# Scores with 64-row contraction: a second transpose and quadrant-to-quadrant copies by DMA, in an attention and feed-forward kernel

## The chip, the cores and the metric

The kernel runs on one core of one Trainium2 chip. The metric is the time of one execution on the device in microseconds (us). The other engines named here are VectorE (DVE), ScalarE (ACT), GpSimd (POOL) and SyncE (SP), which issues most of the DMAs; TensorE is PE, and its weight loads are PEld.

Ratios are the mean time of one kernel's fast runs over the mean of the other's fast runs of the same rounds, so they are not quite the ratio of the medians quoted beside them. A bracket after a ratio is its 95% interval.

## The reference

```python
# q, k, v: [8 batches, 8 heads, 576, 64]; w_in [512, 2048], w_out [2048, 512]
q_d, k_d, v_d = (mean over 4 neighbouring positions of q, k, v)      # 144 positions
out_down  = softmax(q_d @ k_d.T / 8) @ v_d, each row repeated 4 times
out_local = softmax(q @ k.T / 8 where |i - j| < 4) @ v
x = (out_down + out_local), heads side by side                        # [4608, 512]
h = x @ w_in
return (h * sigmoid(1.702 * h)) @ w_out                               # float32
```

## The kernel before

Tokens go through the feed-forward part in nine groups of 512. A group has 64 matmuls of 128x512 on `w_in` and 64 on `w_out`. Between them, at fixed step numbers (`POS`), lies the attention of the batch that comes next, so that TensorE has dense work while the other engines prepare. "Batch 3's group" below is the group that carries the attention of batch 3; its start is the first `w_in` matmul.

A batch has two head groups of four heads. q and k of four heads lie on 128 partitions as bf16. VectorE transposes them in 32-bit units. Each unit is a pair of neighbouring bf16 values, so a head gets 32 partitions, and the pair stands in a last axis `a` of size 2. The contraction over 64 is therefore done as two accumulating matmuls over 32 rows. The downsampled q and k are pooled by GpSimd from the transposed tile.

```python
def prep_1(name, b, qd):
    store, dst = {"k": (kf, kT), "q": (qf, qT)}[name]
    tt = work.tile([128, S, 2], BF16, ...)
    t32 = tt.rearrange("p t a -> p (t a)").bitcast(FP32)
    nc.vector.transpose(out=..., in_=...)          # one of 128x576 32-bit units
    dst[b, qd] = tt

def scores(b, qd):
    for i in range(5):
        for a in range(2):
            for par in range(2):
                for r in range(4):                 # 80 matmuls of 32 rows
                    nc.tensor.matmul(sp[r // 2][...],
                        lhsT=kT[b, qd][32*r : 32*r+32, k0 : k0 + 64, a],
                        rhs=qT[b, qd][32*r : 32*r+32, q0 : q0 + 60, a],
                        start=(a == 0), stop=(a == 1), ...)
# scores_d: the same for the downsampled part, 24 matmuls of 32 rows
# ... cut ...
for g in range(n_groups):
    b = g + 1
    # ... g == 0 cut ...
    if b > 2:
        load_v4(b)                  # six DMAs on the sync queue, 192 KB each
    prep_qk(b, 0)                   # VectorE: two transposes
    pool_qk(b, 0)                   # GpSimd: k and q of head group 0
    load_qk(b + 1, ...)             # GpSimd issues four DMAs
    prep_v(b, nc.gpsimd)            # GpSimd: cast of v
    load_v(b + 1)                   # ten DMAs on the sync queue
    prep_qk(b, 1)
    pool_qk(b, 1)
    prep_v4(b, nc.gpsimd)           # GpSimd: pooling of v from v4, written to vd
    # ... mm1 and mm2 with the attention's matmuls at POS ...
```

GpSimd works through its part of one group in exactly this order. Its last result, `vd`, is read by the "AV-down" matmuls at step 42.

The softmax here doesn't subtract the row's maximum and nothing guards it: scores larger than these inputs give would overflow.

Of the kernel before, what the change touches and what calls it, by code (L numbers as in the profile page):

```python
# [8 lines left out]
FP32 = mybir.dt.float32  # L9
BF16 = mybir.dt.bfloat16  # L10
AF = mybir.ActivationFunctionType
ALU = mybir.AluOpType
# [7 lines left out]
def kernel(  # L20
# [9 lines left out]
    nc = tc.nc  # L30
    B, H, S, D = q.shape
    SD = S // 4
# [6 lines left out]
    inv_sqrt_d = 1.0 / math.sqrt(D)  # L39
    KSTART = (0, 56)  # L40
    QSTART = (0, 60)

    ctx.enter_context(
        tc.manual_schedule(engines={ET.PE, ET.Activation, ET.DVE, ET.Pool, ET.SP})
# [19 lines left out]
    eds = [persist.tile([128, 2, 464], BF16, name=f"ed{i}") for i in range(2)]  # L64
    v4 = persist.tile([128, 3, HP, 4 * D], FP32, name="v4")
    kdT = [persist.tile([128, 160, 2], BF16, name=f"kdT{i}") for i in range(NQ)]

    PA = [psum.tile([128, 2, 512], FP32, name=f"pa{i}") for i in range(3)]
    PM = [psum.tile([128, 512], FP32, name=f"pm{i}") for i in range(2)]
# [2 lines left out]
    def ps_tile(n=None):  # L72
        if n is None:
            n = turn["a"] % 3
            turn["a"] += 1
        return PA[n]
# [44 lines left out]
    def fill():  # L121
        nc.vector.memset(wz, 0.0)
        for t in kdT:
            nc.vector.memset(t[:, SD:160, :], 0.0)
        for t in vbs:
            nc.vector.memset(t[:, :, :, 64:65], 1.0)
        for t in vds:
            nc.vector.memset(t[:, :, :, 64:65], 4.0)
        for t in es:
            nc.vector.memset(t[:, :, 300:304], 1.0)  # L130
        for t in eds:
            nc.vector.memset(t[:, :, 432:464], 1.0)
# [122 lines left out]

    def prep_1(name, b, qd):
        store, dst = {"k": (kf, kT), "q": (qf, qT)}[name]
        tt = work.tile([128, S, 2], BF16, name=f"{name}T{qd}", tag=f"{name}T{qd}", bufs=1)
        t32 = tt.rearrange("p t a -> p (t a)").bitcast(FP32)
        nc.vector.transpose(  # L260
            out=t32.rearrange("p (i c) -> p c i", c=18),
            in_=store[b, qd].bitcast(FP32).rearrange("p (c d) -> p c d", c=18),
        )
        dst[b, qd] = tt

    def prep_qk(b, qd):
        prep_1("k", b, qd)
        prep_1("q", b, qd)

    def pool_qk(b, qd, names="kq"):  # L270
        for name, src in (("k", kT), ("q", qT)):
            if name not in names:
                continue
            sv = src[b, qd].rearrange("p (j f) a -> p j f a", f=4)
            t1 = work.tile([128, SD, 2, 2], FP32, name="pq", tag="pq")
            nc.gpsimd.tensor_tensor(  # L276
                out=t1, in0=sv[:, :, 0:2, :], in1=sv[:, :, 2:4, :], op=ALU.add
            )
            if name == "k":
                dst = kdT[qd][:, 0:SD, :]  # L280
            else:
                t = work.tile([128, SD, 2], BF16, name=f"qdT{qd}", tag=f"qdT{qd}", bufs=1)
                qdT[b, qd] = t
                dst = t
            nc.gpsimd.tensor_tensor(
                out=dst, in0=t1[:, :, 0, :], in1=t1[:, :, 1, :], op=ALU.add
            )

    def prep_v(b, eng, i=slice(0, 5), h=slice(0, H)):
        cp = eng.copy if eng is nc.scalar else eng.tensor_copy  # L290
        cp(out=vbs[b % 2][:, i, h, 0:D], in_=vf[b][:, i, h])  # L291
# [47 lines left out]

    def scores(b, qd, barred=False):  # L340
        sp = [ps_tile(), ps_tile()]
        if barred:
            bar_others(sp)
        for i in range(5):
            for a in range(2):
                for par in range(2):
                    for r in range(4):
                        rows = slice(32 * r, 32 * r + 32)
                        k0 = 114 * i + KSTART[par]
                        q0 = 114 * i + QSTART[par]  # L350
                        nc.tensor.matmul(  # L351
                            sp[r // 2][64 * par : 64 * par + 64, r % 2, 60 * i : 60 * i + 60],
                            lhsT=kT[b, qd][rows, k0 : k0 + 64, a],
                            rhs=qT[b, qd][rows, q0 : q0 + 60, a],
                            start=(a == 0 and not barred),
                            stop=(a == 1 or barred),
                            tile_position=(32 * r, 64 * par),
                            skip_group_check=barred,
                        )
        return sp  # L360

    def scores_d(b, qd, sd=None):
        sd = sd or ps_tile()
        bank = sd if sd is PM else [sd[:, u, :] for u in range(2)]
        for kc in range(3):
            for a in range(2):
                for r in range(4):
                    rows = slice(32 * r, 32 * r + 32)
                    j = r % 2
                    nc.tensor.matmul(  # L370
                        bank[r // 2][64 * j : 64 * j + 64, SD * kc : SD * kc + SD],
                        lhsT=kdT[qd][rows, 48 * kc : 48 * kc + 64, a],
                        rhs=qdT[b, qd][rows, :, a],
                        start=(a == 0), stop=(a == 1),
                        tile_position=(32 * r, 64 * j),
                    )
        return sd
# [428 lines left out]
    for g in range(n_groups):  # L806
        b = g + 1
        if g == 0:
            prep_qk(1, 0)
            pool_qk(1, 0)  # L810
            prep_qk(1, 1)
            load_v(1, gate=after(w_out_bf[0:1, 0, 0:1], nc.vector))
            pool_qk(1, 1)
            nc.gpsimd.tensor_copy(
                out=w_out_bf[0:1, 8, 0:1], in_=vf[1][0:1, 3, 0, 0:1]
            )
            load_w_out(2)
            load_w_out(3)
            for i in range(5):
                prep_v(1, nc.gpsimd, i=slice(i, i + 1))  # L820
            for qd in range(NQ):
                load_qk(2, qd)
            loads_2()
        elif b < B:
            if b > 2:
                load_v4(b)
            prep_qk(b, 0)
            pool_qk(b, 0)
            if b + 1 < B:
                for qd in range(NQ):  # L830
                    load_qk(b + 1, qd)
            prep_v(b, nc.gpsimd)
            if b + 1 < B:
                load_v(b + 1)
            prep_qk(b, 1)
            pool_qk(b, 1)
            prep_v4(b, nc.gpsimd)
        steps = {}
        if b < B:
            for n, f in zip(POS if g else POS_0, attention(b, None if g else (1, 2))):  # L840
                steps.setdefault(n, []).append(f)
            if g == 0:
                steps.setdefault(VDP_0, []).append(lambda: prep_vd_pe(1, PA[2]))
        gT = new_gT() if g else gT0
        mm1(g, gT, steps, 0 if g else 6)
        mm2(g, gT, {n - 16: f for n, f in steps.items() if n >= 16})
# [30 lines left out]
```

## Time and profile before

| | before |
|---|---|
| median of the runs beside the changed kernel | 332.29 us (over four runs; the first took 1751.61 us and is in this median but not in the ratio; the other three took 331.47, 331.97 and 332.61) |
| span of the profiled run | 329.5 us |
| TensorE busy | 308.0 us, 93% |
| GpSimd / VectorE busy | 138.9 us (42%) / 130.2 us (40%) |
| groups of batches 3 to 6, from start to start | 33.71, 33.53, 33.40, 34.31 us (mean 33.74) |

From the page of the kernel before come its busy times, its clock row in 40 slices (tenths of the full TensorE clock) and the shares of the chain of work that ended last.

```profile
PE 308.0 (93%) x4987; PEld 157.9 (48%) x5043; DVE 130.2 (40%) x215; ACT 184.1 (56%) x322; POOL 138.9 (42%) x168
...
PEclk9997999999999999999999999999999999999999
...
PE 87%; issue 4%; SPq 3%; ACT 2%; DVE 2%; DMA 1%; DVEq 0%; ACTq 0%
```

TensorE is the limit: it is busy nearly all the time, the clock is full except for one slice, and 87% of the chain is TensorE. The next fence is the timeline of batch 3's group, cut. Its columns are start, duration (both us), engine, line and operation, output and input; in brackets stands the idle time before it and what ended that.

```profile
102.18 11.39 PE L618 MATMUL pm<-xT,w_in_bf 128*128 128x512 bf16 x51
...
102.65 1.26 DVE L260 STREAM_TRANSPOSE kT<-kb 128x576 f32<-128x576 f32 x1
...
103.46 3.08 SPq L226 DMA_DIRECT2D v<-in_v_dram  x6
...
103.98 1.15 POOL L276 TENSOR_TENSOR pq<-kT 128x576 f32<-128x576 bf16 x1 [15.95 <-DVE kT L260]
...
107.06 0.67 POOL L285 TENSOR_TENSOR qdT<-pq 128x288 bf16<-128x288 f32 x1
...
113.50 0.84 PE L351 MATMUL pa<-qT,kT 32*64 32x60 bf16 x80
...
114.14 0.59 PE L370 MATMUL pa<-qdT,kdT 32*64 32x144 bf16 x24
...
121.22 0.84 POOL L300 TENSOR_TENSOR vd<-v 112x256 bf16<-112x256 f32 x1
...
124.61 0.32 PE L431 MATMUL pa<-vd,ed 48*64 48x65 bf16 x17
```

The matmuls that the change improves: 80 of them take 114.14 - 113.50 = 0.64 us, 8.0 ns each. GpSimd starts 1.80 us into the group, released by the first transpose, works without a gap until 122.06, and TensorE reads its last result at 124.61. The slack is 2.55 us in a group of 33.7 us.

### The profile page before, as it was taken

The page shows a single profiled execution, that of the slowest core. Times are in us where ns is not written, and L with a number is a line of the kernel's source. Part 1 is how long each engine was busy: PE and PEld are TensorE (multiplying, and loading weights), DVE is VectorE, ACT ScalarE, POOL GpSimd, SP SyncE. Part 2 cuts the span into 40 slices and gives each one's busy share as a digit, 9 for nine tenths or more (in the row PEclk, how much of TensorE's full clock was granted, in tenths as well). Part 3 has the DMA queues.
Part 4 walks back from the last instruction along what each step waited for, and adds up shares of the span by engine and source line. Part 5 has one row for each costly group of instructions (what it writes and reads, how often), then busy time and mean ns, then how long its engine had stood idle before and what let it go on. Part 6 is the DMA issues. An engine that isn't in the chain of part 4 may idle for free.

```text
span 329.5 us, 11220 instructions
## 1 busy us (share of the span) xinstructions
PE 308.0 (93%) x4987; PEld 157.9 (48%) x5043; DVE 130.2 (40%) x215; ACT 184.1 (56%) x322; POOL 138.9 (42%) x168
## 2 busy tenths in 40 slices
PE   8767999789999999999999999998999999999995
PEld 3444455445554455455544555455444544444444
DVE  4870512770468036802771277225730560000000
ACT  2552773375936683667367746674566646415611
POOL 7890844049603970298029901990098000000000
PEclk9997999999999999999999999999999999999999
DMA  7999979999814991398339922993180110011011
GB/s 126 184 188 208 171 151 183 196 210 236 191 39 132 205 207 39 116 193 171 102 100 200 200 83 86 196 195 105 40 172 2 60 41 32 2 72 56 2 62 65
DMA packets 63552, 41.36 MB, mean 126 GB/s; under 512 B 44048, under 2 KB 54416, under 8 KB 63504
## 3 DMA queue, kind: packets, MB, share of 16 engines
q1 hardware_dynamic: 55056, 26.95, 35.8%
q0 software_dynamic: 8304, 13.63, 23.9%
q8 instruction: 39, 0.64, 0.9%
q14 instruction: 9, 0.07, 0.1%
q10 hardware_dynamic: 144, 0.07, 0.1%
HBM read 44.83 MB, written 9.44 MB: 165 GB/s over the span
## 4 chain that ended last, share of the span: by engine, by line
PE 87%; issue 4%; SPq 3%; ACT 2%; DVE 2%; DMA 1%; DVEq 0%; ACTq 0%
PE pm L618 35%; PE pm L674 33%; PE pa L351 3%; SPq L214 3%; PE pa L618 2%; PE pa L431 2%; PE pa L409 2%; PE pa L370 2%; PE pa L458 2%; PE pa L674 2%; DMA vf<-in_v_dram 1%; PE pm L689 1%; PE pa L484 1%; ACT vd L321 0%; PE pa L312 0%
## 5 line engine op out<-in xcount | busy, mean ns | idle before, releaser
L618 PE MATMUL pm<-xT,w_in_bf 128*128 128x512 bf16 x528 | 120.3, 380 | 1.4 <-DVE xT L561 0.7
L674 PE MATMUL pm<-w_out_bf,gT 128*128 128x512 bf16 x493 | 114.1, 379 | 5.4 <-issue 5.2
L629 ACT ACTIVATE gT<-pm 128x512 bf16<-128x512 f32 x136 | 81.0, 598 | 45.2 <-PE pm L618 45.2
L618 PEld LDWEIGHTS <-w_in_bf 128*128 128x128 bf16 x576 | 55.8, 98 | 68.4 <-issue 2.5
L674 PEld LDWEIGHTS <-gT 128*128 128x128 bf16 x560 | 51.7, 98 | 59.5 <-issue 0.2
L276 POOL TENSOR_TENSOR pq<-kT 128x576 f32<-128x576 bf16 x16 | 18.5, 1157 | 105.0 <-DVE kT L260 96.1
L395 DVE TENSOR_TENSOR es<-es,mask 128x600 bf16<-128x600 bf16 x28 | 20.6, 749 | 92.0 <-ACT es L381 91.2
L659 ACT ACTIVATE osb<-pm 128x512 f32<-128x512 f32 (+2 forms) x35 | 20.7, 592 | 40.2 <-PE pm L674 36.1
L534 ACT COPY od<-pa 128x384 f32<-128x384 f32 (+1 forms) x56 | 18.4, 412 | 32.4 <-DVE y L444 18.7
L444 DVE TENSOR_TENSOR y<-pa,rc 128x896 bf16<-128x896 f32 x32 | 34.9, 1092 | 1.1
L555 DVE TENSOR_TENSOR xT<-pa,od 128x570 bf16<-128x570 f32 x28 | 21.1, 753 | 12.0 <-ACT od L534 11.9
L381 ACT ACTIVATE es<-pa 128x600 bf16<-128x600 f32 x32 | 19.8, 668 | 7.0 <-PE pa L351 6.8
L297 POOL TENSOR_TENSOR v<-v 112x512 f32<-112x512 f32 x18 | 22.8, 1265 | 0.0
L661 DVE TENSOR_SCALAR osb<-pm 128x128 f32<-128x128 f32 x1 | 0.3, 292 | 55.3 <-ACT osb L659 55.3
L260 DVE STREAM_TRANSPOSE kT<-kb 128x576 f32<-128x576 f32 x16 | 20.0, 1249 | 2.0 <-DMA kb<-in_k_dram 2.0
L260 DVE STREAM_TRANSPOSE qT<-qb 128x576 f32<-128x576 f32 x16 | 19.8, 1239 | 0.9 <-DMA qb<-in_q_dram 0.7
L276 POOL TENSOR_TENSOR pq<-qT 128x576 f32<-128x576 bf16 x16 | 18.4, 1148 | 0.0
L291 POOL CAST vb<-vf 128x2560 bf16<-128x2560 f32 (+1 forms) x11 | 17.6, 1618 | 0.0
L442 DVE RECIPROCAL rc<-pa 128x14 f32<-128x14 f32 x32 | 7.7, 240 | 21.7 <-PE pa L431 21.7
L351 PE MATMUL pa<-qT,kT 32*64 32x60 bf16 x1280 | 14.0, 203 | 1.5 <-issue 1.5
L351 PEld LDWEIGHTS <-kT 32*64 32x64 bf16 x1280 | 11.8, 104 | 6.7 <-issue 5.5
L300 POOL TENSOR_TENSOR vd<-v 112x256 bf16<-112x256 f32 x18 | 13.7, 759 | 1.4
(90 smaller groups left out, 247.0 us busy)
## 6 DMA issues: line engine op xcount, KB each, us to landing
vf<-in_v_dram SPq DMA_DIRECT2D x80, 128.0 KB, 4.7
out_dram<-osb SPq DMA_DIRECT2D x35, 256.0 KB, 2.1
v<-in_v_dram SPq DMA_DIRECT2D x36, 192.0 KB, 6.1
kb<-in_k_dram POOLq DMA_DIRECT2D x16, 288.0 KB, 6.8
qb<-in_q_dram POOLq DMA_DIRECT2D x16, 288.0 KB, 7.1
w_out_bf<-in_moe_w_out_dram POOLq DMA_DIRECT2D x4, 512.0 KB, 12.1
w_in_bf<-in_moe_w_in_dram POOLq DMA_DIRECT2D x2, 512.0 KB, 5.7
w_in_bf<-in_moe_w_in_dram POOLq DMA_DIRECT2D x1, 1024.0 KB, 10.7
```

The costliest lines, as they stand in the source:

```text
L260: nc.vector.transpose(out=t32.rearrange("p (i c) -> p c i", c=18), in_=store[b, qd].bitcast(FP32).rearrange("p (c d) -> p c d", c=18),)
L276: nc.gpsimd.tensor_tensor(out=t1, in0=sv[:, :, 0:2, :], in1=sv[:, :, 2:4, :], op=ALU.add)
L297: eng.tensor_tensor(out=t1[0:112], in0=x[:, :, 0:2, :], in1=x[:, :, 2:4, :], op=ALU.add)
L351: nc.tensor.matmul(sp[r // 2][64 * par : 64 * par + 64, r % 2, 60 * i : 60 * i + 60], lhsT=kT[b, qd][rows, k0 : k0 + 64, a], rhs=qT[b, qd] ...
L381: nc.scalar.activation(out=es[2 * qd + u][:, :, 0:300], in_=sp[u][:, :, 0:300], func=AF.Exp, scale=inv_sqrt_d,)
L395: nc.vector.tensor_tensor(out=ev, in0=ev, in1=mask, op=ALU.mult)
L444: nc.vector.tensor_tensor(out=y, in0=ov[:, :, :, 0:D], in1=rc.to_broadcast([128, 2, 7, D]), op=ALU.mult,)
L555: eng.tensor_tensor(out=sub(xT[hp], t0 + 3, (57, 2), (114, 5), (1, 57)), in0=sub(x, 3, (509, 2), (57, 5), (1, 57)), in1=sub(od, 3, (57, 2) ...
L618: nc.tensor.matmul(acc, lhsT=w_in_bf[:, dmc, ffc * 128 : (ffc + 1) * 128], rhs=xT[dmc][:, g * TG : g * TG + TG], start=(dmc == 0), stop=(d ...
L629: nc.scalar.activation(out=gT[:, ffc, :], in_=acc, func=AF.Silu, scale=GELU_SCALE)
L659: eng.activation(out=osb, in_=ap, func=AF.Copy, scale=1.0 / GELU_SCALE)
L674: nc.tensor.matmul(ops[t], lhsT=gT[:, ffc, t * 128 : (t + 1) * 128], rhs=w_out_bf[:, ffc, :], start=(ffc == 0), stop=(ffc == n_ffc - 1),)
```

## The change

The intent is to contract over 64 rows at once, with half as many score matmuls. From batch 2 on each q/k tile is transposed twice into two planes. In plane 0 the odd elements of heads on even quadrants, and in plane 1 the others, are brought into the neighbouring quadrant of 32 partitions by small DMAs that write one bf16 element off, so that position `a = 0` holds even elements in one quadrant and odd elements in the next: 64 rows for one head.

```diff
+    ROWS64 = 2
     def prep_1(name, b, qd):
-        tt = work.tile([128, S, 2], BF16, ...)
-        nc.vector.transpose(...)
-        dst[b, qd] = tt
+        n = 2 if b >= ROWS64 else 1
+        tt = work.tile([128, 2, S, 2], BF16, ...)
+        for x in range(n):
+            nc.vector.transpose(...)               # the same, into tt[:, x]
+        if n == 2:
+            for x in range(2):
+                f = tt[:, x].rearrange("p t a -> p (t a)")
+                for r in range(2):
+                    src = 64 * r + 32 * x
+                    to = 64 * r + 32 * (1 - x)
+                    nc.sync.dma_start(
+                        out=f[to : to + 32, 0 : 2 * S - 1], in_=f[src : src + 32, 1 : 2 * S]
+                    )
+        dst[b, qd] = tt if n == 2 else tt[:, 0]
     # pool_qk: same sizes, reads a = 0 of both planes (so it waits for the copies); pq has 1 buffer, not 2
     # scores:   40 matmuls of 64 rows in place of 80 of 32
     # scores_d: 12 matmuls of 64 rows in place of 24 of 32
     # ... cut ...
             prep_v(b, nc.gpsimd)
+            prep_qk(b, 1)
             if b + 1 < B:
                 load_v(b + 1)
-            prep_qk(b, 1)
             pool_qk(b, 1)
```

Per batch this adds four transposes and 16 copies of 71.9 KB, 96 copies in all, on the sync queue.

More of the change, by code (lines that the diff above doesn't have):

```diff
@@ L66 @@
     kdT = [persist.tile([128, 160, 2], BF16, name=f"kdT{i}") for i in range(NQ)]
+    kdP = [persist.tile([128, 2, 160], BF16, name=f"kdP{i}") for i in range(NQ)]
     PA = [psum.tile([128, 2, 512], FP32, name=f"pa{i}") for i in range(3)]
@@ L124, in fill @@
             nc.vector.memset(t[:, SD:160, :], 0.0)
+        for t in kdP:
+            nc.vector.memset(t[:, :, SD:160], 0.0)
         for t in vbs:
@@ L257, in prep_1 @@
         store, dst = {"k": (kf, kT), "q": (qf, qT)}[name]
-        tt = work.tile([128, S, 2], BF16, name=f"{name}T{qd}", tag=f"{name}T{qd}", bufs=1)
-        t32 = tt.rearrange("p t a -> p (t a)").bitcast(FP32)
-        nc.vector.transpose(
-            out=t32.rearrange("p (i c) -> p c i", c=18),
-            in_=store[b, qd].bitcast(FP32).rearrange("p (c d) -> p c d", c=18),
-        )
-        dst[b, qd] = tt
+        n = 2 if b >= ROWS64 else 1
+        tt = work.tile([128, 2, S, 2], BF16, name=f"{name}T{qd}", tag=f"{name}T{qd}", bufs=1)
+        for x in range(n):
+            t32 = tt[:, x].rearrange("p t a -> p (t a)").bitcast(FP32)
+            nc.vector.transpose(
+                out=t32.rearrange("p (i c) -> p c i", c=18),
+                in_=store[b, qd].bitcast(FP32).rearrange("p (c d) -> p c d", c=18),
+            )
[7 more added lines that the diff above has]
+                        out=f[to : to + 32, 0 : 2 * S - 1], in_=f[src : src + 32, 1 : 2 * S]
+                    )
+        dst[b, qd] = tt if n == 2 else tt[:, 0]
     def prep_qk(b, qd):
@@ L273, in pool_qk @@
                 continue
+            if b >= ROWS64:
+                sv = src[b, qd].rearrange("p x (j f) a -> p (x j) f a", f=4)[:, :, :, 0]
+                t1 = work.tile([128, 2 * SD, 2], FP32, name="pq", tag="pq", bufs=1)
+                nc.gpsimd.tensor_tensor(
+                    out=t1, in0=sv[:, :, 0:2], in1=sv[:, :, 2:4], op=ALU.add
+                )
+                if name == "k":
+                    dst = kdP[qd][:, :, 0:SD]
+                else:
+                    dst = work.tile([128, 2, SD], BF16, name=f"qdT{qd}", tag=f"qdT{qd}", bufs=1)
+                    qdT[b, qd] = dst
+                t1 = t1.rearrange("p (x j) f -> p x j f", x=2)
+                nc.gpsimd.tensor_tensor(
+                    out=dst, in0=t1[:, :, :, 0], in1=t1[:, :, :, 1], op=ALU.add
+                )
+                continue
             sv = src[b, qd].rearrange("p (j f) a -> p j f a", f=4)
-            t1 = work.tile([128, SD, 2, 2], FP32, name="pq", tag="pq")
+            t1 = work.tile([128, SD, 2, 2], FP32, name="pq", tag="pq", bufs=1)
             nc.gpsimd.tensor_tensor(
@@ L341, in scores @@
         sp = [ps_tile(), ps_tile()]
+        if b >= ROWS64:
+            for j in range(2):
+                for i in range(5):
+                    for par in range(2):
+                        for u in range(2):
+                            rows = slice(64 * u, 64 * u + 64)
+                            k0 = 114 * i + KSTART[par]
+                            q0 = 114 * i + QSTART[par]
+                            nc.tensor.matmul(
+                                sp[u][64 * par : 64 * par + 64, j, 60 * i : 60 * i + 60],
+                                lhsT=kT[b, qd][rows, j, k0 : k0 + 64, 0],
+                                rhs=qT[b, qd][rows, j, q0 : q0 + 60, 0],
+                                start=True, stop=True,
+                                tile_position=(64 * u, 64 * par),
+                            )
+            return sp
         if barred:
@@ L363, in scores_d @@
         sd = sd or ps_tile()
+        if b >= ROWS64:
+            for kc in range(3):
+                for j in range(2):
+                    for u in range(2):
+                        rows = slice(64 * u, 64 * u + 64)
+                        nc.tensor.matmul(
+                            sd[64 * j : 64 * j + 64, u, SD * kc : SD * kc + SD],
+                            lhsT=kdP[qd][rows, j, 48 * kc : 48 * kc + 64],
+                            rhs=qdT[b, qd][rows, j, :],
+                            start=True, stop=True,
+                            tile_position=(64 * u, 64 * j),
+                        )
+            return sd
         bank = sd if sd is PM else [sd[:, u, :] for u in range(2)]
```

## The prediction

> **What bounds it now.** The page: TensorE busy 93% of a 329.5 us span, and 87% of the chain that ended last, most of it the two 128x512 lines. The timeline: a group of batches 2 to 7 takes about 34 us and TensorE never waits long. The matmuls that change are small: 80 local-score matmuls start at 113.50 and their successor at 114.14, 8 ns each; the 24 downsampled-score matmuls take about 0.5 us.
>
> **What it removes.** Per head group 80+24 matmuls become 40+12. 64x64 tiles already run in the AV line: 20 matmuls in 0.18 us, 9 ns each. So 40 take about 0.37 us, saving 0.27; the downsampled ones save perhaps 0.1. Twelve calls: about 4.5 us (1.4%), if TensorE stays the limit.
>
> **What it adds.** Per batch four more transposes on VectorE (1.25 us each; 1.1 from start to start) and 16 copies of 32 rows x 2.3 KB on the sync DMA queue. Pooling on GpSimd keeps its size (1.15 + 0.67 us) but now waits for the copies.
>
> **Where that lands.** A new critical path, through GpSimd. In batch 3's group (timeline) the last merge ends at 102.7; transposes start at 102.65; GpSimd starts pooling at 103.98 and works without a gap until 122.06 (pooling, four load issues, V cast, pooling, V pooling). The AV matmuls that read its last result start at 124.61: slack 2.55 us; in batches 2 to 6 it is 2.4 to 2.6, in batch 7 4.6. GpSimd starting later than that stalls TensorE.
>
> It will start much later:
> - the sync queue issues the last store at 103.0 and six v4 loads at 103.5 to 106.5, still ahead of the copies in the changed program's order;
> - in that order each DMA also waits for the completion of the one eight before it: the third and fourth k copies wait for the first two v4 loads, the q copies for the other four. These land 4.8 to 5.9 us after issue, at 108.3 to 112;
> - a DMA needs at least 2.0 us from issue to landing (fastest store). The Trainium skill, "DMA: Bandwidth & Descriptors", Anatomy of one DMA, also gives about 2.0 us fixed cost; the trace agrees.
>
> So k copies land near 111.2, q copies near 113.3. Pooling of head group 0 ends near 115.1 instead of 107.67: 7.5 us later, and everything behind it too. TensorE waits about 1 us at the downsampled scores, the rest at AV: 7.5 - 2.55 = 4.9 us per group. Faster scores only lengthen the wait.
>
> Sum: batches 3 to 6, 4 x 4.9 = 19.6; batch 7, 2.9; batch 2 (no v4 load ahead, but four stores until 73.05) about 3.5. Total 26; a little off because the landings are pessimistic: +23 us.
>
> **Predicted: 356 us, 343 to 366 (8 in 10).** Faster by over 2%: 0.03; within 2%: 0.06; slower: 0.91.
>
> **Signs.** Right: TensorE idle 3 to 5 us per group just before the AV-down matmuls, put down to GpSimd's vd; GpSimd's idle before pooling ends on the copies, about 8 us into the group; score matmuls about 9 ns apart. Wrong: TensorE still 93% busy, span near 325.
>
> **What would make it wrong.** Copies landing within 2.5 us of the transposes (then -1%). Or worse: small copies at odd 2-byte offsets being slow; or the clock dropping in the waits: the skill, "TensorE: Matmul & The Clock Gate", Part 1, tells of half clock after an idle window of about 3.4 us; the slices show one dip (0.7), after a 2.9 us idle at 23.5 us.

Two statements of it do not stand as they are. The least landing time of 2.0 us holds for stores of 256 KB (fastest 2.02 us); the last store of the kernel before, of 64 KB, landed in 1.55 us, so "at least" is not shown. And batch 2 does have v4 loads ahead: `loads_2()` puts them at the end of group 0 (see the account of the prediction below).

## The result, and the profile after

| | before | after |
|---|---|---|
| median | 332.29 us | 387.17 us (383.25 to 387.99, four runs) |
| ratio of fast runs | | 1.1638 [1.1536, 1.174] |
| span of the profiled run | 329.5 us | 384.9 us |
| TensorE busy | 308.0 us | 324.1 us |
| TensorE idle (span less busy) | 21.5 us | 60.8 us |
| mean granted clock of TensorE | 0.995 | 0.929 |
| groups of batches 3 to 6 | mean 33.74 us | 44.06, 41.55, 43.82, 41.93 us (mean 42.84) |

The change cost 55 us where 23 had been foretold. The page of the kernel after shows the same three rows:

```profile
PE 324.1 (84%) x4363; PEld 160.5 (42%) x4419; DVE 162.0 (42%) x241; ACT 183.7 (48%) x322; POOL 142.0 (37%) x168
...
PEclk9896999998899896999899897998899699999999
...
PE 60%; POOL 20%; DMA 8%; issue 6%; SPq 4%; DVE 1%; ACT 1%; POOLq 0%; ACTq 0%; DVEq 0%
```

TensorE executes 624 fewer matmuls and is busy 16 us longer. That is no contradiction: the clock row has many slices of 0.6 to 0.8 now, and matmuls at a lower clock take longer (ten of 128x512 took 4.28 us after a wait, where they had taken 2.32; the lines are shown below). In the chain, GpSimd, which had no share in the row before, has 20%, and DMA has gone from 1% to 8%.

The timeline of batch 3's group after, in the columns explained above, answers to the one of before. The group starts at 115.29.

```profile
115.29 11.39 PE L678 MATMUL pm<-xT,w_in_bf 128*128 128x512 bf16 x51
...
115.95 2.34 DVE L266 STREAM_TRANSPOSE kT<-kb 128x576 f32<-128x576 f32 x2
...
116.54 2.85 SPq L230 DMA_DIRECT2D v<-in_v_dram  x6
...
119.49 2.48 SPq L276 DMA_DIRECT2D kT<-kT  x4
...
122.06 3.20 SPq L276 DMA_DIRECT2D qT<-qT  x4
...
125.67 1.15 POOL L292 TENSOR_TENSOR pq<-kT 128x576 f32<-128x576 bf16 x1 [23.17 <-DMA kT<-kT]
...
126.61 0.54 PE L381 MATMUL pa<-qT,kT 64*64 64x60 bf16 x40
...
129.59 0.38 PE L416 MATMUL pa<-qdT,kdP 64*64 64x144 bf16 x12 [2.44 <-POOL qdT L301]
...
137.10 1.38 POOL L292 TENSOR_TENSOR pq<-qT 128x576 f32<-128x576 bf16 x1 [1.28 <-DMA qT<-qT]
...
139.38 0.38 PE L416 MATMUL pa<-qdT,kdP 64*64 64x144 bf16 x12 [0.91 <-ACT es L441]
...
143.77 0.22 PE L491 MATMUL pa<-vd,ed 48*64 48x65 bf16 x4 [1.65 <-POOL vd L331]
...
145.02 0.73 POOL L331 TENSOR_TENSOR vd<-v 112x256 bf16<-112x256 f32 x1
145.80 0.38 PE L491 MATMUL pa<-vd,ed 48*64 48x65 bf16 x10 [1.80 <-POOL vd L331]
```

GpSimd begins 10.38 us into the group (before: 1.80), released by the k copies. Its last result is ready 30.46 us into the group (before: 19.88). TensorE waits four times: for the pooled q, for ScalarE, and twice for `vd`. The median time of the first four k copies from issue to landing is 5.0 us (the view of DMA issues for 119.4 to 122.0 us; count, KB each, us to landing):

```profile
kT<-kT SPq DMA_DIRECT2D x4, 71.9 KB, 5.0
```

In the trace the last v4 load lands at 124.75 us, and the first three k copies right behind it, at 124.96, 125.16 and 125.32. The waits of the two engines over the whole run say the same (engine, output, line and releaser; then us in total, times, longest us). TensorE after, and then SyncE's queue, where copies wait for v4 loads to land:

```profile
PE pa L491 <- POOL vd L331: 17.0, 10, 1.8
PE pa L416 <- POOL qdT L301: 15.4, 7, 2.6
...
SPq L276 <- DMA v<-in_v_dram: 6.2, 14, 0.7
```

The table by stretches gives the two groups as a whole. Its columns are the stretch, its length, busy time of PE, PEld, DVE, ACT and POOL (instructions in brackets), the granted clock, the DMA engines' mean busy share and GB/s. Batch 3's group before:

```profile
102.18:135.90 33.72, 32.81 (x595) 16.92 (x601) 16.35 (x25) 20.95 (x36) 17.52 (x19) 1.00 0.68 142
```

Batch 3's group after, then one stretch with the v4 loads under way and one with the k copies as well, and then two neighbouring stretches around the wait for `vd`:

```profile
115.29:159.30 44.01, 36.15 (x490) 17.50 (x496) 21.56 (x29) 20.85 (x36) 18.16 (x19) 0.88 0.67 136
...
118.00:119.00 1.00, 1.00 (x7) 0.42 (x5) 1.00 (x2) 0.65 (x2) 0.00 (x0) 1.00 0.91 286
...
122.00:123.00 1.00, 1.00 (x6) 0.47 (x5) 1.00 (x2) 0.73 (x2) 0.00 (x0) 1.00 1.12 218
...
141.00:144.40 3.40, 1.35 (x32) 0.60 (x31) 0.80 (x1) 1.01 (x1) 3.32 (x4) 0.98 1.37 206
144.40:147.80 3.40, 1.67 (x54) 1.32 (x55) 1.49 (x3) 0.00 (x0) 1.26 (x2) 0.50 0.19 59
```

Of the 10.3 us that this group is longer, TensorE's idle time is 7.0 (44.01 - 36.15 = 7.86 against 33.72 - 32.81 = 0.91) and longer busy time is 3.3, at a mean clock of 0.88. The DMA engines have a busy share above 1 from 119 to 124 us, that is, all 16 are full, with the six v4 loads (1.18 MB) and the copies. And right after a stretch in which TensorE was busy for only 1.35 of 3.40 us, the granted clock falls to 0.50. The ten `w_out` matmuls behind the first AV block show it, after and then before:

```profile
147.16 4.28 PE L734 MATMUL pm<-w_out_bf,gT 128*128 128x512 bf16 x10 [0.33 <-issue]
...
125.67 2.32 PE L674 MATMUL pm<-w_out_bf,gT 128*128 128x512 bf16 x10 [0.16 <-issue]
```

### The profile page after: what moved, and what is told of

It reads as the page before. It is cut to its first block, busy times and chain, and to the rows that moved or that the text cites. A ratio compares the mean times of both kernels' runs of the same rounds, so it can differ in the third digit from the quotient of the medians.

```text
span 384.9 us, 10241 instructions
## 1 busy us (share of the span) xinstructions
PE 324.1 (84%) x4363; PEld 160.5 (42%) x4419; DVE 162.0 (42%) x241; ACT 183.7 (48%) x322; POOL 142.0 (37%) x168
## 4 chain that ended last, share of the span: by engine, by line
PE 60%; POOL 20%; DMA 8%; issue 6%; SPq 4%; DVE 1%; ACT 1%; POOLq 0%; ACTq 0%; DVEq 0%
PE pm L734 24%; PE pm L678 22%; POOL v L328 5%; POOL pq L292 5%; SPq L276 4%; DMA qT<-qT 3%; DMA kT<-kT 3%; POOL vd L331 3%; PE pa L678 2%; PE pa L491 2%; DMA qb<-in_q_dram 2%; POOL vb L322 2%; POOL qdT L301 2%; PE pa L518 2%; PE pa L469 1%
## 5 line engine op out<-in xcount | busy, mean ns | idle before, releaser
L678 PE MATMUL pm<-xT,w_in_bf 128*128 128x512 bf16 x528 | 129.1, 399 | 1.9 <-DVE xT L621 0.7
L734 PE MATMUL pm<-w_out_bf,gT 128*128 128x512 bf16 x493 | 122.3, 399 | 6.1 <-issue 6.0
L292 POOL TENSOR_TENSOR pq<-kT 128x576 f32<-128x576 bf16 x12 | 13.9, 1160 | 144.9 <-DMA kT<-kT 120.8
L455 DVE TENSOR_TENSOR es<-es,mask 128x600 bf16<-128x600 bf16 x28 | 25.7, 942 | 89.3 <-ACT es L441 88.9
L504 DVE TENSOR_TENSOR y<-pa,rc 128x896 bf16<-128x896 f32 x32 | 34.9, 1092 | 1.1
L266 DVE STREAM_TRANSPOSE kT<-kb 128x576 f32<-128x576 f32 x28 | 32.9, 1243 | 2.7 <-DMA kb<-in_k_dram 2.1
L266 DVE STREAM_TRANSPOSE qT<-qb 128x576 f32<-128x576 f32 x28 | 32.8, 1237 | 0.8 <-DMA qb<-in_q_dram 0.8
L491 PE MATMUL pa<-vd,ed 48*64 48x65 bf16 x640 | 14.5, 202 | 17.6 <-POOL vd L331 17.0
L615 DVE TENSOR_TENSOR xT<-pa,od 128x570 bf16<-128x570 f32 x28 | 21.1, 753 | 11.4 <-ACT od L594 11.3
L416 PE MATMUL pa<-qdT,kdP 64*64 64x144 bf16 x144 | 5.0, 243 | 17.8 <-POOL qdT L301 15.4
L491 PEld LDWEIGHTS <-ed 48*64 48x64 bf16 x640 | 11.2, 113 | 18.8 <-issue 18.8
L292 POOL TENSOR_TENSOR pq<-qT 128x576 f32<-128x576 bf16 x12 | 14.1, 1174 | 4.2 <-DMA qT<-qT 3.5
## 6 DMA issues: line engine op xcount, KB each, us to landing
kT<-kT SPq DMA_DIRECT2D x48, 71.9 KB, 3.6
qT<-qT SPq DMA_DIRECT2D x48, 71.9 KB, 2.3
```

What stands on the lines that cost most here:

```text
L266: nc.vector.transpose(out=t32.rearrange("p (i c) -> p c i", c=18), in_=store[b, qd].bitcast(FP32).rearrange("p (c d) -> p c d", c=18),)
L292: nc.gpsimd.tensor_tensor(out=t1, in0=sv[:, :, 0:2], in1=sv[:, :, 2:4], op=ALU.add)
L455: nc.vector.tensor_tensor(out=ev, in0=ev, in1=mask, op=ALU.mult)
L491: nc.tensor.matmul(o[64 * pos : 64 * pos + 64, j, c0 : c0 + 65], lhsT=Ed[64 * j : 64 * j + 48, u, q0 : q0 + 64], rhs=vd[64 * j : 64 * j + ...
L504: nc.vector.tensor_tensor(out=y, in0=ov[:, :, :, 0:D], in1=rc.to_broadcast([128, 2, 7, D]), op=ALU.mult,)
L615: eng.tensor_tensor(out=sub(xT[hp], t0 + 3, (57, 2), (114, 5), (1, 57)), in0=sub(x, 3, (509, 2), (57, 5), (1, 57)), in1=sub(od, 3, (57, 2) ...
```

## The experiments

Fourteen kernels were run; each shares one chip with runs of the kernel before. The comparison with the reference is weak here: inputs are a tenth of a standard normal, so the scores are near zero and the softmax is almost flat, and wrong scores hardly show. Four kernels below are wrong (said where it is so).

Theory A: the copies land late, GpSimd starts late, and TensorE waits for GpSimd. Rivals: B, the copies cost through the traffic that they add or because of their form (small, odd offset, many); C, the rest of the change (bigger tiles, second transposes, fewer buffers, the moved `load_v`); D, the clock, which falls in the waits, is the main part.

The kernel before: 331.64 us.

### e1_inactive: the changed program with the new path switched off

```diff
-    ROWS64 = 2
+    ROWS64 = 8
```

> The changed kernel with the row threshold set to 8, so that no batch takes the new path; what stays is the single buffer of the pooling tile, the two extra fills, the doubled tiles and the later V load in the queue. Main theory (the loss is the wait for the copies): equal to before, 331 to 335 us. The changed kernel's group 0, where the new path is not used, ended 3.0 us later than before's; if that is a lasting side effect of what stays, this run shows about 335; if it is the clock's window falling differently in that one profile, about 332.

Measured: 329.79 us, ratio 1.0011 [0.991, 1.011]. The bigger tiles, the single `pq` buffer and the moved `load_v` cost nothing that shows (the interval is about 1% to either side).

### e2_no_copies: everything but the copies (wrong result)

```diff
-                for r in range(2):
-                    ...
-                    nc.sync.dma_start(out=f[to : to + 32, ...], in_=f[src : src + 32, ...])
```

> The changed kernel with the copies taken out, all else kept (wrong result on purpose: the odd elements are missing). Main theory (wait for the copies): TensorE's matmuls are about 1 us per group shorter, GpSimd starts pooling only about 1.1 us later than before (the second transpose), within its slack of 2.5 us: 325 to 331 us, mean clock back at 0.99. Rival (doubled transposes on VectorE, or the new strides on GpSimd, or the 64-row matmuls, cost the time): stays above 345 us.

Measured: 326.39 us, ratio 0.9857 [0.979, 0.992]. In the timeline of this kernel, batch 3's group (start 99.4) has GpSimd starting at 2.9 us and done at 21.8 us:

```profile
102.27 1.15 POOL L283 TENSOR_TENSOR pq<-kT 128x576 f32<-128x576 bf16 x1 [13.98 <-DVE kT L266]
...
120.34 0.83 POOL L322 TENSOR_TENSOR vd<-v 112x256 bf16<-112x256 f32 x1
```

So the second transposes delay GpSimd by 1.1 us at the start and 1.9 us at the end, which the slack of 2.55 us swallows, and the groups become shorter (32.89 us against 33.74). The whole loss of 55 us comes in with the copies, and theory C falls. The gain that the change was made for exists, too: about 0.9 us per group.

### e3_unwaited: the copies run, but nobody reads what they write

```diff
-    ROWS64 = 2
+    ROWS64 = 8
+    EXTRA = 2          # second transposes and copies from batch 2 on
-                        out=f[to : to + 32, ...], in_=f[src : src + 32, ...]
+                        out=g[to : to + 32, ...], in_=f[src : src + 32, ...]   # plane 0 -> plane 1
-        dst[b, qd] = tt if n == 2 else tt[:, 0]
+        dst[b, qd] = tt[:, 0]                                                # 32-row path
```

> The old 32-row arithmetic (correct result), but from batch 2 on with the same 16 copies per batch on the same queue, read from the transposed tile and written to a tile that nobody reads. Main theory (only the waiting hurts, not the occupancy): 331 to 337 us, GpSimd starting within 2 us of the group's start. Rival (96 more DMAs on the queue and the 16 engines slow the loads that others need): above 345 us.

Measured: 332.75 us, ratio 1.0064 [0.9993, 1.0136]. The page's list of DMA issues (count, KB each, median us from issue to landing) shows that the same 96 copies ran, and landed even later than in the changed kernel (3.6 and 2.3 us there):

```profile
kT<-kT SPq DMA_DIRECT2D x48, 71.9 KB, 6.1
qT<-qT SPq DMA_DIRECT2D x48, 71.9 KB, 5.4
```

Copies that take 6 us and that nobody waits for cost 0.6%, and 1.4% at the upper end of the interval. With e2 this settles the first question: neither their traffic nor their issue costs the time by itself, but the wait for them.

### e4_warm: dummy matmuls keep TensorE busy in the waits

```diff
 def scores_d(...):
+        for n in range(10):
+            nc.tensor.matmul(sd[:, n % 2, :], lhsT=wz[:, 0:128], rhs=wz, start=True, stop=True)
 def av_local(...):
+        if b >= ROWS64 and hp == 0:
+            # 16 more of the same
```

> The changed kernel with dummy 128x512 matmuls where TensorE waited: 10 before each downsampled-score block, 16 before the first AV block, in the same PSUM tiles that are written next. If the half clock is a separate term, the clock rises from 0.93 to above 0.97 and the ten matmuls after the first AV block take 2.3 us instead of 4.3: 2 us per group, 370 to 378 us in all. If the half clock is only a mark of the waiting and costs nothing, 383 to 390 us as the changed kernel.

Measured: 378.65 us, ratio 1.146 [1.1389, 1.1531], slightly above the range. The mean clock was 0.994, so the half clock was indeed gone, and GpSimd ended as late as in the changed kernel (30.25 us into batch 3's group; there 30.46). The groups of batches 3 to 6 took 41.89, 41.79, 41.70 and 41.42 us. The difference of the ratios, 0.018, is 6 us (the two intervals together allow 2 to 10); that of the medians is 8.5. The dummies ended up to 0.4 us after `vd` was ready, so they cost a little themselves. The half clock is a real term, of some 6 to 9 us, and theory D is not the main part.

The kernel before: 331.54 us.

### e5_order: the copies of head group 0 ahead of the v4 loads

```diff
+            prep_qk(b, 0)
             if b > 2:
                 load_v4(b)
-            prep_qk(b, 0)
```

> The changed kernel with the six v4 loads issued after the copies of head group 0 instead of before them; nothing else moves. Main theory: in batches 3 to 7 the first k copies no longer wait behind the v4 loads and for their landing, so GpSimd starts pooling about 6 us after the group's start instead of 10.4; part comes back because the copies of head group 1 now stand behind the v4 loads. Estimate 352 to 364 us; batch 2's group, which has no v4 load ahead, stays about 10 us too long. Rival (the copies need that long by themselves, whatever stands ahead): 380 to 388 us.

Measured: 383.95 us, ratio 1.1558 [1.1512, 1.1604]: a miss by 20 us. GpSimd did start early, but then stood still. Its timeline in batch 3's group (start 112.8):

```profile
118.94 1.15 POOL L292 TENSOR_TENSOR pq<-kT 128x576 f32<-128x576 bf16 x1 [18.94 <-DMA kT<-kT]
...
132.69 1.14 POOL L292 TENSOR_TENSOR pq<-kT 128x576 f32<-128x576 bf16 x1 [4.91 <-DMA kT<-kT]
...
142.89 0.72 POOL L331 TENSOR_TENSOR vd<-v 112x256 bf16<-112x256 f32 x1
```

It starts 6.15 us into the group, waits 4.91 us for the k copies of head group 1, and ends at 30.8 us, no earlier than in the changed kernel. Those copies were issued from 122.99 to 125.4, now behind the v4 loads and beside the q and k loads of the next batch, which GpSimd itself issues once head group 0 is pooled. The lateness was moved, not removed. The Trainium skill, "DMA: Bandwidth & Descriptors", Issuing engines are not separate DMA queues, says that DMAs started by the scalar, sync or GpSimd engine end on the same 16 DMA engines and interleave. The trace agrees: these four copies of the sync queue took a median of 7.7 us from issue to landing beside loads of two queues.

### e6_short: a quarter of the bytes (wrong result)

```diff
-        out=f[to : to + 32, 0 : 2 * S - 1], in_=f[src : src + 32, 1 : 2 * S]
+        out=f[to : to + 32, 0 : 287], in_=f[src : src + 32, 1 : 288]
```

> The changed kernel with the same 96 copies, but each of 287 instead of 1151 elements per row (wrong result on purpose). If the number of DMAs counts (0.5 to 0.6 us of issue each and the wait for the eighth before), hardly anything changes: 376 to 387 us, issues still above 0.45 us. If the bytes count, the copies land earlier and the time falls to 360 to 374 us.

Measured: 385.88 us, ratio 1.1612 [1.155, 1.167]. The copies' own bytes do not matter here. One issue on the sync queue still took 0.51 to 0.58 us where nothing blocked it.

### e7_early: head group 0 transposed and copied one batch ahead

```diff
-    ROWS64 = 2
+    ROWS64 = 3
     # q and k of batch b + 2, not b + 1, are loaded in group b
+            elif b + 1 < B:
+                steps.setdefault(14, []).append(lambda c=b + 1: prep_qk(c, 0))
```

> The same copies, taken off the path: from batch 3 on (batch 2 keeps the 32-row path) the transposes and copies of head group 0 are made one batch ahead, just after the scores of the batch before have freed the tile, and q/k are loaded one batch earlier; head group 1 stays where it was, since GpSimd needs it some 8 us later. Main theory (only the wait for the copies costs): 325 to 331 us, GpSimd starting its pooling without waiting for a copy, scores about 1 us shorter per group: 0 to 2% faster than before. Rival (the copies cost wherever they stand): above 345 us.

Measured: 340.52 us, ratio 1.0252 [1.0215, 1.0289], where 325 to 331 had been expected. Two of its six runs were slow, among them the profiled one. About 85% of the loss is gone. Not all of that is the time that the first set of copies gets: batch 2, whose group alone was 10.2 us longer in the changed kernel, keeps the 32-row path here. What was left, as the trace of the slow run has it: in batch 3's group GpSimd waited 7.88 us for the k copies of head group 1, which stood behind v4 loads.

### e8_aligned: the copies without the odd offset (wrong result)

```diff
-        out=f[to : to + 32, 0 : 2 * S - 1], in_=f[src : src + 32, 1 : 2 * S]
+        out=f[to : to + 32, 0 : 2 * S], in_=f[src : src + 32, 0 : 2 * S]
```

> The changed kernel with the copies made from offset 0 and over the whole row of 1152 elements, so that source, target and length are multiples of four bytes (wrong result on purpose). If the odd offset is what makes a copy's issue take 0.53 to 0.58 us where a store's takes 0.33 us, the issue falls to about 0.35 us, 3 us per group are saved, and the time is 362 to 374 us. If not, 383 to 389 us and the issue stays.

Measured: 386.18 us, ratio 1.1647 [1.1588, 1.1706]. An issue of four took 2.44 to 2.48 us where nothing blocked it, as before. The offset of two bytes, one of the doubts of the prediction, costs nothing that shows.

The kernel before: 330.28 us.

### e9_spread: e7, with the v4 loads at the end of the group before

```diff
     # on top of e7_early:
-            if b > 2: load_v4(b)                       # at the group's start
+                steps.setdefault(56, []).append(lambda c=b + 1: load_v4(c))
     # load_qk moved behind prep_v4
```

> The early version again (40 of the copies one batch ahead, 40 at the group's start), with the big loads taken out of the copies' way: v4 is loaded late in the group before, q/k are loaded after GpSimd's last work of the group, GpSimd pools head group 0 and casts V ahead of the group's start. Theory as it now stands (the copies are slow because four to sixteen of them take 0.5 to 0.6 us of issue each and land in 2 to 8 us when the 16 DMA engines are full of loads; it hurts where GpSimd waits for them): GpSimd gets the k copies of head group 1 by 9 us after the group's start instead of 11 to 16, its last V pooling ends before 21 us, TensorE does not wait: 324 to 330 us, so 0.5 to 2% faster than before. Rival (the copies cost by their number wherever they stand): 338 us or more, as the early version.

Measured: 336.13 us, ratio 1.0165 [1.0114, 1.0216]: a miss, 324 to 330 had been expected. GpSimd was done 16.4 to 17.7 us into the groups of batches 3 to 7, earlier than in the kernel before. The last two groups, which carry no q/k loads, took 32.46 and 32.47 us, a microsecond less than before. Some of the others were held up: batch 2's group took 38.74 us, and TensorE had single idle times of 0.8 to 2.6 us that are put down to "issue", that is, to no wait that the profile shows.

### e10_half: two copies in place of four (wrong result)

```diff
-                for r in range(2):
+                for r in range(1):
```

> The changed kernel with every second copy left out (48 of 96, the rows of heads 2 and 3; wrong result on purpose). A quarter of the bytes changed next to nothing (385.9 us), so if it is the number of DMAs, with 0.5 to 0.6 us of issue each and the wait for the eighth before, half the number brings GpSimd's start from about 10.4 to 8 or 9 us after the group's start and the second half's copies in time: 366 to 377 us. If the number does not matter either, and only the v4 and q/k loads that fill the DMA engines do: 380 us or more.

Measured: 383.68 us, ratio 1.1605 [1.1539, 1.1671]: a miss, expected was 366 to 377. The issue was halved (two copies in 1.22 us), and GpSimd started as late as ever. The timeline of batch 3's group (start 111.5), SyncE's queue and GpSimd:

```profile
115.74 1.22 SPq L276 DMA_DIRECT2D kT<-kT  x2
...
121.64 1.15 POOL L292 TENSOR_TENSOR pq<-kT 128x576 f32<-128x576 bf16 x1 [22.88 <-DMA kT<-kT]
```

The two copies had been issued by 116.96 and were waited for until 121.64. So with the v4 loads ahead, neither bytes (e6) nor alignment (e8) nor number (e10) decides when they land. That leaves little of theory B for this place, and what is left is what the copies stand behind: 1.18 MB of v4 data. At the 218 to 286 GB/s that the trace of the changed kernel shows in this stretch, that is an estimated 4.1 to 5.4 us. Whether the number counts once the loads are gone, e10 does not test.

### e11_order32: the load order of e9 without the new path

```diff
     # e9_spread with
-    ROWS64 = 3
+    ROWS64 = 8
+    EARLY = 3
```

> Control for the spread version: the same order of loads and transposes, but the old 32-row path in all batches, so no second transposes and no copies. If the spread version's gain comes from the 64-row matmuls (about 1 us per group in five groups), this one is at before, 329 to 333 us, and some 5 us slower than the spread version. If the new order itself gains, it is as fast as the spread version or faster.

Measured: 334.67 us, ratio 1.0117 [1.0066, 1.0168]. A good part of e9's remaining loss is thus the price of its load order; batch 2's group is 38.6 us here as well. But the expected 5 us between the two did not come. Only the last two groups show the saving, 32.46 us in e9 against 33.39 here. In batches 3 to 5 e9's groups are as long as these or up to 0.4 us longer, so something in the new path, not isolated, still costs there what the matmuls save.

The prediction had been wrong and one point was open: how much of the loss is the v4 data ahead of the copies. The fourth call (before: 331.28 us) and the fifth (331.76 us) went to that and to a version that might win.

### e12_v4late: the changed kernel with nothing but the v4 loads moved

```diff
-            if b > 2:
-                load_v4(b)
+            elif b + 1 < B:                            # at step 56 of the group before
+                steps.setdefault(56, []).append(lambda c=b + 1: load_v4(c))
```

> The changed kernel with the v4 loads of batches 3 to 7 moved to late in the group before, so that they stand neither before nor between the copies; q/k loads, copies and all else as in the changed kernel. If the v4 loads (1.2 MB, some 5 us of the full DMA engines) are the bulk of what the copies wait for, GpSimd starts pooling at about 5.5 to 6.5 us after the group's start and gets the second half's copies without a wait, its V pooling ends at about 25 us instead of 30, and the time is 350 to 364 us, with batch 2's group still about 10 us too long. If it is the q/k loads or the copies themselves, GpSimd waits again at the second half and the time stays above 375 us.

Measured: 367.12 us, ratio 1.107 [1.1026, 1.1114], somewhat above the range. The timeline of batch 3's group (start 114.2):

```profile
116.15 2.49 SPq L276 DMA_DIRECT2D kT<-kT  x4
...
120.25 1.15 POOL L292 TENSOR_TENSOR pq<-kT 128x576 f32<-128x576 bf16 x1 [18.87 <-DMA kT<-kT]
...
132.51 1.15 POOL L292 TENSOR_TENSOR pq<-qT 128x576 f32<-128x576 bf16 x1 [1.52 <-DMA qT<-qT]
...
140.09 0.73 POOL L331 TENSOR_TENSOR vd<-v 112x256 bf16<-112x256 f32 x1
```

With the v4 loads out of the way, GpSimd starts 6.08 us into the group in place of 10.38, and ends at 26.65 in place of 30.46. That is worth 19 us (by the ratios) to 20 us (by the medians) of the 55, the part of the half clock that goes with it included (clock 0.958). So the copies had stood behind the v4 loads, and in two ways. The first copy is issued 1.99 us into the group in place of 4.20, since the six v4 issues no longer precede it on the queue. And from the end of the fourth issue to GpSimd's start it takes 1.6 us in place of 3.7. Each is about half of the 4.3 us. The rest is the bare price of the copies: second transposes, 2.5 us for four issues, and 1.6 us from the end of the last issue to GpSimd's start still make GpSimd 6.5 us late (mean of batches 3 to 6), against a slack of 2.55.

### e13_from4: e9's order and the new path from batch 4 on

```diff
-    ROWS64 = 2
+    ROWS64 = 4
     # and e9_spread's order from batch 4 on
```

> The spread version with the new path and the new order only from batch 4 on: batch 2's group is before's, so that the group of 38.7 us that the spread version and its 32-row control both had there goes away. Groups of batches 4 to 7 at about 32.5 us against 33.4 before: 326 to 330 us, 0.3 to 1.3% faster than before on the same chip. If the loads of the new order cost as much wherever it begins, 332 us or more.

Measured: 335.36 us, ratio 1.0089 [1.003, 1.0147]: a miss, 326 to 330 had been expected. The last two groups took 32.46 and 32.47 us again, the others 34.7 to 37.6.

### e14_loads_mid: e9 with other places for the loads

```diff
     # e9_spread with load_qk before prep_v4, and
-                steps.setdefault(56, []).append(lambda c=b + 1: load_v4(c))
+                steps.setdefault(34, []).append(lambda c=b + 1: load_v4(c))
```

> The spread version with the q/k loads some 6 us earlier (before the V pooling instead of after it) and the v4 loads for the next batch some 5 us earlier, so that fewer big loads are in flight while TensorE runs its many small AV and transpose matmuls. In the spread version the groups with q/k loads lost 0.8 to 2.6 us there with no releaser named in the trace (the groups of batches 6 and 7, without such loads, took 32.5 us). If those idle stretches come from the loads in flight, they shrink, all groups from batch 3 on come to 32.5 to 33 us, and the time is 324 to 330 us, 0.5 to 2% faster than before. If they stay, 333 to 337 us as the spread version, and their cause stays open.

Measured: 332.76 us, ratio 1.003 [0.9977, 1.0083], the same as the kernel before, and outside both expected ranges. Four groups, those of batches 3, 4, 6 and 7, are now at 32.5 to 33.0 us. Two are not, batch 2's (37.04) and batch 5's (36.88). The timeline of TensorE in batch 5's group:

```profile
193.21 0.25 PE L491 MATMUL pa<-vd,ed 48*64 48x65 bf16 x5 [2.54 <-issue]
193.62 4.01 PE L734 MATMUL pm<-w_out_bf,gT 128*128 128x512 bf16 x10 [0.16 <-issue]
```

A gap of 2.54 us in the middle of a row of small matmuls, with no releaser, and after it ten matmuls at half clock (4.01 us; 2.32 at full clock). Such gaps appear in e9, e11 and e13, too, in groups that have loads in them, and move with the loads. What they are is not settled. No version with a right result beats the kernel before.

## Why the prediction was right or wrong

**Right: the mechanism and the direction.** The prediction said that the copies would put GpSimd on the critical path and that TensorE would wait for `vd`. The chain (GpSimd 20%), the waits (17.0 us for `vd`, 15.4 us for the pooled q), and e2 with e3 show it: without the copies 326.4 us, with copies that nobody waits for 332.8 us. The foretold sign held too: in batches 2 to 6 TensorE waited 3.4 us per group for `vd` (3 to 5 foretold). The split was less well seen: for the pooled q it waited 2.1 to 3.4 us per group, not about 1. The saving was right as well: 40 matmuls of 64 rows take 0.35 us from their start to that of the next line in e9 (head group 0), 8.75 ns each (9 foretold; 80 took 0.64 us before), and groups without waits become about 0.9 us shorter (0.75 foretold).

**Wrong: the size of the sum, term by term.** The foretold sum was 26 us, cut to 23 because the landings were thought pessimistic; that cut went the wrong way. The step that failed is the landing of the copies: it was put at 2 us after their issue, and with the v4 loads ahead it took about 5. The other missing terms are the growth of the delay on its way through GpSimd, the clock, and batch 2. The measured groups:

| term | foretold | measured |
|---|---|---|
| batches 3 to 6, per group | +4.9 | +9.1 (42.84 - 33.74) |
| ... GpSimd's last result, later by | 7.5 | 9.8 (mean of 10.6, 8.9, 10.4, 9.4) |
| ... slack to subtract | 2.55 | 2.55 |
| ... rest of the group, half clock included | 0 | 1.8 (9.1 less 9.8 - 2.55) |
| batch 7 | +2.9 | +5.9 (no wait for `vd`; see 5 below) |
| batch 2 | +3.5 | +10.2 (GpSimd later by 11.5) |
| start of batch 2's group | 0 | +3.0 |
| sum (four times the first line, and the last three) | 26 | 55.5 (rounded terms; the spans differ by 55.4) |

The last rise, in the start of batch 2's group, is not a term of the change: it lay between 65.0 and 70.0 us from kernel to kernel, and e1 shows no lasting cost of the changed program. Counted on TensorE, the 9.1 us per group of batches 3 to 6 are 6.5 us more idle time and 2.6 us more busy time, though the score matmuls had become shorter.

1. *"k copies land near 111.2, q copies near 113.3"*, that is 9.0 and 11.1 us into the group, is the step that failed first. The k copies were waited for until 10.1 to 11.4 us. The prediction had let the third and fourth of them wait, before their issue, for the first two v4 loads to land, by the rule that a DMA waits for the eighth before it, and had then given them 2 us to land. In the trace no copy waits longer than 0.7 us for that (6.2 us in 14 waits of the whole run), and the k copies of batch 3 not at all. They were all issued by 121.97 us and landed about 5 us after their issue, behind the last v4 load. So the wait lies in the landing, not before the issue. e12, which takes these loads away, brings GpSimd's start back to 6.1 us, and e10, which halves the copies, does not. GpSimd's start was 8.8 us later than before (mean of batches 3 to 6), where 7.5 had been foretold for the end of its first pooling.

2. *"Pooling of head group 0 ends ... 7.5 us later, and everything behind it too"* assumed that the delay is handed on unchanged. It grew from 8.8 to 9.8 us on the mean: in batch 3 GpSimd waited another 1.28 us for the q copies of head group 1, and some of its operations were slower (1.49 us for one that took 1.26).

3. *The clock* stood in the list of doubts and not in the sum. The ten `w_out` matmuls after the wait took 4.28 us in batch 3 and 2.32 before. e4 gives some 6 to 9 us for the whole run. It is less than the 16 us by which TensorE's busy time grew, presumably because the stretch at half clock after the first wait only shortens the next one; no run isolates that.

4. *"Batch 2 (no v4 load ahead, but four stores until 73.05) about 3.5"* is wrong in its premise. `loads_2()` puts batch 2's six v4 loads at the end of group 0, ahead of these copies. SyncE's queue around the start of batch 2's group (70.04) in the changed kernel:

```profile
68.98 4.23 SPq L230 DMA_DIRECT2D v<-in_v_dram  x6
73.31 2.58 SPq L724 DMA_DIRECT2D out_dram<-osb  x4
76.65 2.67 SPq L276 DMA_DIRECT2D kT<-kT  x4
```

The first copy was issued 6.6 us into the group, and the fourth issue ended at 9.3. The last v4 load landed at 9.05, three of the k copies at 11.3 to 11.7, and GpSimd started at 11.84 us. It is the same queue of loads as in the later groups, with four stores added. e12 moves only the v4 loads of batches 3 to 7 and leaves this group at 44.4 us; it says nothing about these six.

5. *Batch 7* was to lose what exceeds its slack of 4.6 us at AV. TensorE did not wait for `vd` there at all. It waited 0.9 us for q copies and 2.4 us for the pooled q, and its busy time grew by 2.4 us (34.9 against 32.5) at a mean clock of 0.91:

```profile
302.23 0.57 PE L416 MATMUL pa<-qdT,kdP 64*64 64x144 bf16 x12 [2.39 <-POOL qdT L301]
```

**The doubts that were none.** Odd offsets (e8) and the copies' bytes (e6) cost nothing that shows with the v4 loads ahead, and there their number (e10) does not matter either. e12 does not clear the number: without the loads, the four issues take 2.5 of the 6.1 us until GpSimd starts.

**Open.** Why a copy takes 0.5 us to issue; what share of the loss the issue time has by itself, apart from landing, since e12 leaves both, and no run halves the copies with the v4 loads out of the way or issues them from another engine's queue; and the gaps without a releaser in e9 to e14.

## What to carry to other kernels

Before a change puts a DMA between two engines, find the consumer's slack (here 2.55 us in a group of 34) and hold the DMA's whole price against it: the issue of all copies one after the other, the landing, and everything queued ahead on the same DMA engines; the saving on the busy engine (here under 1 us per group) comes after that. An engine that is idle 58% of the time can have as little slack as this, so read when it works. When a wait of some microseconds falls on TensorE, count the half clock behind it as well, and when an experiment moves one delayed transfer, look for where the queue makes the next one late.

## What the Trainium skill lacked or had wrong

- "DMA: Bandwidth & Descriptors", Anatomy of one DMA: its breakdown of the fixed cost, made for the GpSimd path, gives the sequencer's dispatch as about 50 ns and calls the generation of descriptors small and variable. Here each q or k load that GpSimd issued held its queue for 0.54 to 0.69 us. Each copy from partitions to partitions held the sync queue for 0.51 to 0.58 us where nothing blocked it, whether it moved 71.9 KB or a quarter of it (e6) and with or without an odd offset (e8).
- The same page, Issuing engines are not separate DMA queues, calls the time to initiate a DMA usually small relative to the DMA. Here the issue of four copies (2.5 us) took longer than the fastest copy from issue to landing (1.96 us).
- The same section is right that all these DMAs share engines, but it has no figure for how late a small copy becomes. In batch 3, behind six loads of 192 KB, the k copies of head group 0 were waited for until 10.4 us into the group, and without these loads until 6.1 us (e12); about half of the difference is the issue of those loads ahead on the same queue.
- "TensorE: Matmul & The Clock Gate", Part 1, has the half clock after an idle window of about 3.4 us. In the trace a stretch of that length with TensorE busy for 1.35 of 3.40 us, its longest idle time 1.65 us, was followed by one at a clock of 0.50. An entirely idle window is not needed here; how little work is enough to keep the clock the page does not say, and these runs do not settle it.
